# Four more attention units handled as one burst each, a new search of the order of work, and one store a half at the end of a Trainium2 attention and MoE kernel

## The chip, the cores and the metric

The kernel runs on one core of one Trainium2 chip. The metric is the device time of one execution in microseconds (us), as the median of several runs. The core has a matrix engine (TensorE, "PE" in the profile), a vector engine (DVE), a scalar engine (ACT), GpSimd (POOL) and a queue engine (SP), which here only issues DMAs. ACT also issues a few.

## The reference, cut to what matters

Random-feature attention over 8 batches of 8 heads with 576 tokens of 64 numbers and 128 features, and behind it a gated pair of projections:

```python
proj = np.einsum('bhsd,md->bhsm', x, omega)
h = proj - np.sum(x * x, axis=-1, keepdims=True) / 2.0
phi = np.exp(h - np.max(h, axis=-1, keepdims=True)) / np.sqrt(m)   # for q and for k
kv = np.einsum('bhsm,bhsd->bhmd', k_p, v)
z = np.sum(k_p, axis=2)
num = np.einsum('bhsm,bhmd->bhsd', q_p, kv)
den = np.einsum('bhsm,bhm->bhs', q_p, z)[..., None] + 1e-06
x = (num / den).transpose(0, 2, 1, 3).reshape(4608, 512)
out = ((x @ w_a) * (x @ w_b)) @ w_out        # w_a, w_b: 512 x 1536; w_out: 1536 x 512
```

## The kernel before, in words

**Two kinds of work on one matrix engine.** The attention is cut into 32 units, u = 4b + hp: batch b and pair of heads hp. So units 7 to 10 are (1,3), (2,0), (2,1) and (2,2). A unit projects k and q on the features (`four`, matmuls at L641 into `ppk` and `ppq`), forms kv (`kv_burst`, L918), and later the numerator (`num`, L990 for 512 tokens and L993 for the last 64). These matmuls use a part of the matrix engine's array at a time (the profile prints 64*64 or another shape behind the operation). The projections behind them ("MoE") run in 9 blocks of 512 tokens on the whole array (128*128): blocks 0 and 1 as plain matmuls (`moe_block`: L1327 for `pa` and `pb`, L1137 for the output `o`, 12 steps a block), blocks 2 to 8 by a scheme with sums of tiles and fewer products (`moe_block7`: the products at L1418 go into the banks `p0` and `p1` of PSUM, and DVE adds them at L1428). Each matmul is three: high and low halves of both operands, without low times low.

**The output of blocks 7 and 8** has the class `Out7`. Its products (L1206) collect in banks of their own, except for the product with key 1 (function `one`): this one goes into `p1`, DVE adds it to a sum in SBUF (`add`, L1216), and after that the next L1418 product may take `p1`. At the end of block 8 `store` writes four tiles `oc` of 128 x 512 numbers, the last one in two parts, as soon as each part has its last sum (L1213).

**What sets the order.** The program isn't in the order of its source. A planner (class `Graph`) collects all operations with their costs, and a list scheduler puts those of each engine in order by due times. Tables of numbers steer it: `PLACE` says at which MoE step a unit's matmuls stand, and `SHIFT` and `TILT` move single operations, by their number, in due time and in priority. `MERGED` lists units whose matmuls stand together: such a unit's burst takes the two banks that the next step's `pa` and `pb` will use (`pab`), holds its numerator of the unit ahead, kv and the projections, and goes to PE as one piece with MoE matmuls ahead and behind. A unit that isn't merged has several smaller pieces between MoE matmuls. In `JOIN` are units whose numerator is cut in two halves to share banks with kv. `LOWP` lists weight conversions of which one step is done by POOL. `XL` gives the steps from which the 64-token tails of all batches (block 8's x) may be loaded and split. `mm()` is the planner's price of a matmul.

**Stores.** A DMA is described by nested dimensions on both sides. The sums of the attention, `zx`, are stored 28 times to `zdr` as 8 rows of 32 numbers (L443, called from L893); each tile `oc` of the end in rows of 256 numbers.

Of the kernel before, what the change touches and what calls it, by code (L numbers as in the profile page):

```python
# [18 lines left out]
P = 128  # L19
B, H, S, D, M = 8, 8, 576, 64, 128  # L20
NHP = H // 2
NU = B * NHP
E, FF = H * D, 1536
# [3 lines left out]
HM = SM // 2  # L27
NFP = NF // 2
B1 = 2
TL = S - SM  # L30
# [6 lines left out]
EPS = 1e-6 * M  # L37
KS = NHP

CFG = dict(TWIN=(0, 1, 2, 3, 4, 6, 7), LOWP=(1, 6, 10, 12, 13, 16, 19, 20, 21, 22, 25, 33, 34), SQP=('natk_0_0', 'natk_0_1', 'natq_0_0', 'natq_0_1', 'natq_0_3'), BW=365.0, DLAT=(1500, 2600), QUEUE=8, XL=(0, 2), JOIN=(6, 7, 8, 9, 10), LOWD=430, SQB=1, GLUE=700, TURNS=99, EDF=("DVE", "ACT", "POOL"), ROUNDS=1, SQUEEZE=1, CAP=("DVE", "ACT", "POOL"), ZS=600, ZB=(1500, 3000, 5000), ZD=(1500, 3000, 4500), HQ=(2500, 4000, 5000), BACK2=(1500, 2500, 4000), TW=(), WAIT=0, RAW=2000, FAST=(0, 1, 2, 3), JOIN0=False, WARM=8, HROOM=["w0", "u1", "w1", "u2", "w2", "u3"], H=3, TURN=(7,), BACK=1500, AT=2, MERGED=(5, 12, 13, 14, 15, 16, 17, 18, 19, 20, 21, 22, 23, 24, 25, 26, 27, 28, 29, 30, 31), SQPE=4, MARGIN=1200, LOAD=2500, SUMS=1400, NATS=(2,), CONV=(22000, 2200))  # L40


PLACE = {4: 3, 5: 4, 6: 7, 7: 9, 8: 10, 9: 12, 10: 14, 11: 18, 12: 20, 13: 21, 14: 27, 15: 29, 16: 33, 17: 35, 18: 38, 19: 41, 20: 45, 21: 47, 22: 50, 23: 54,
         24: 58, 25: 59, 26: 62, 27: 66, 28: 67, 29: 70, 30: 74, 31: 77, 32: 78, 33: 83}


SHIFT = {49: -8000, 89: 1500, 99: -4000, 123: 500, 156: -4000, 179: -1000, 253: 9500, 459: -1000, 558: -2000, 629: 500, 633: -500, 646: -4000, 730: 8000, 749:
         8000, 989: 4500, 995: -8000, 1081: 4000, 1200: 8000, 1207: 4000, 1339: 4000, 1352: 5000, 1483: -8000, 1546: 8000, 1587: 3000, 1957: -8000, 2016:
         1500, 2248: -2000, 2395: -8000, 2854: 3500, 3508: -4000, 3860: -2000, 3940: 6000, 4192: 2000}
TILT = {15: 800, 19: -800, 21: 800, 30: 3000, 34: -800, 58: 3000, 75: -3000, 79: 800, 81: 800, 88: -3000, 105: 800, 109: -800, 115: -3000, 124: 3000, 135:  # L50
# [9 lines left out]


class Buf:
# [35 lines left out]
class Graph:  # L98
# [79 lines left out]
    def dues(self):  # L178
# [16 lines left out]
        for o in self.order:  # L195
            if "PE" in o.eng:
                idle += max(0, o.start - at - 5) * CFG["SQUEEZE"]
                at = o.end
# [11 lines left out]
        while heap:  # L210
            d, _, o = heapq.heappop(heap)
            e = next(iter(o.eng))
            cost = o.end - o.start if o.bytes else o.eng[e]
            if e in CFG["CAP"]:
                now = min(-d, ptr.get(e, inf))
# [12 lines left out]
    def plan(self):  # L228

        self.schedule()  # L230
        for _ in range(CFG["ROUNDS"]):
            self.dues()
            self.schedule()
        for o in self.ops:
            o.shift, o.tilt = SHIFT.get(o.n, 0), TILT.get(o.n, 0)
        self.schedule()
# [9 lines left out]
    def schedule(self):  # L246
# [12 lines left out]
        def entry(o, x, t):  # L259

            t = max(t, free[x] + 112 * (x == "DVE" and o.port == twice == 2))
            if x == "DVE" and o.port and port["POOL"][0] < t:
                t = max(t, port["POOL"][1] - 135)
            elif x == "POOL" and port["DVE"][0] <= t:
                t = max(t, port["DVE"][1] - 140)
            return t
# [20 lines left out]
        while len(done) < len(self.ops):  # L287
            best = None
            for e in engines:
                mine = None  # L290
                for o in ready[e]:
# [3 lines left out]
                    s = entry(o, e, max(o.need, at[0] + 92 * (e == "PE" and at[0] > 0)))  # L295
                    if o.bytes and len(landed) >= CFG["QUEUE"]:
                        s = max(s, landed[-CFG["QUEUE"]] + 100)
                    for x in o.eng:
# [3 lines left out]
                    else:  # L302


                        wait = CFG["WAIT"] if e == "DVE" and 0 <= o.prio < 4000 else 0
                        pr = o.shift + (o.prio if o.due is None or e not in CFG["EDF"] else o.due)
# [45 lines left out]

def mm(n, cols):

    return n * (118.1 if cols == 256 else max(112, 6.9 + 0.4375 * cols))


def mm4(n, cols):
# [24 lines left out]
def tile_attention_moe(ctx: ExitStack, tc: tile.TileContext, kqt, kqtt, kqn, kqnt, vx, omst, idn, wab, wout, out):  # L383
    nc = tc.nc
    SQPE = CFG["SQPE"]
# [10 lines left out]
    g = Graph()  # L396
# [45 lines left out]
    def dma(dst, src):  # L442
        return lambda e: nc.sync.dma_start(dst(), src())  # L443
# [63 lines left out]
    for kind, i, ws in units:  # L507
        n = place[kind, i, ws[0]]
# [26 lines left out]
        if kind == "o":  # L535
# [3 lines left out]
                 nbytes=P * 2 * E * 4)  # L539
# [570 lines left out]
    class Out:  # L1110
# [20 lines left out]
        def mm(self, t, ghl, wo, prio):  # L1131
            b, po, osb, n, h = self.b, self.po[t], self.osb[t // 2], self.n[t], t % 2
            self.n[t] += 1

            def go(e):
                for i, (gi, wi) in enumerate(((0, 0), (0, 1), (1, 0))):
                    nc.tensor.matmul(po.ap[:], ghl.ap[:, gi, t * P:(t + 1) * P], wo.ap[:, wi],  # L1137
                                     start=(n == 0 and i == 0), stop=(n == NF - 1 and i == 2))
            g.op({"PE": mm(3, E)}, go, r=[(ghl, None), (wo, None)], w=[(po, None)], alloc=[po] if n == 0 else [], prio=prio)
            if n < NF - 1:  # L1140
                return
            g.op({"ACT": act(E), "DVE": dve(E)}, copier(lambda: osb.ap[:, h], lambda: po.ap[:]), r=[(po, None)], w=[(osb, h)], alloc=[] if h else [osb], prio=-5)
            g.op({"SP": 330}, dma(lambda: out[b * S + t * P:b * S + (t + 1) * P, :], lambda: osb.ap[:, h]), r=[(osb, h)], prio=-5, nbytes=P * E * 4)
# [26 lines left out]
    class Out7:  # L1170
# [48 lines left out]
        def store(self, o, th, dh, part=None):  # L1219

            b, cols = self.b, slice(HM * dh, HM * dh + HM)
            if b < B:
                r0 = b * S + HM * th
                g.op({"SP": 330}, dma(lambda: out[r0:r0 + HM, cols].rearrange("(t p) c -> p t c", p=P), lambda: o.ap[:]), r=[(o, None)], prio=-5,
                     nbytes=P * E * 4)
                return
            rows = out.rearrange("(n s) c -> n s c", s=S)[4 * th:4 * th + 4, SM:S, cols].rearrange("(t j) r c -> j r t c", j=2)
            tt = slice(0, 2) if part is None else slice(part, part + 1)
            for j, (eng, queue) in enumerate((("SP", nc.sync), ("ACT", nc.scalar))):
                g.op({eng: 330}, lambda e, j=j, queue=queue: queue.dma_start(rows[j][:, tt], o.ap[TL * j:TL * j + TL, tt]),  # L1230
                     r=[(o, part)], prio=-5, nbytes=TL * E * (4 if part is None else 2))

        def items(self, i, C, ghl, Sg, wo, ot):

# [279 lines left out]
    def bursts(step, place, banks):  # L1514

        for u, at in PLACE.items():
            if at == step:
# [5 lines left out]
    for b in range(B + 1):  # L1523
        if b < B1:
            moe_block(b)
        else:
            if b == B:

                for hp in range(NHP):
# [3 lines left out]
                         prio=-20, nbytes=P * SM * 4, deps=[steps[NF * (B - 1) + CFG["XL"][0]]])  # L1533
# [88 lines left out]
```

## Time and profile before

| what | value |
|---|---|
| time, median of 3 runs | 1020.82 us (1020.35 to 1022.02) |
| profiled execution, its own time | 1018.96 us |
| its span | 1017.2 us |
| PE busy | 1006.6 us, 99% |
| DVE busy | 873.1 us, 86% |
| ACT, POOL busy | 574.6 us, 110.7 us |
| granted TensorE clock, mean | 0.999 |

The span is what the trace covers; the execution's time is 1.76 us longer, and the median of the runs 1.86 us longer than that execution. A row of the timeline gives start and length of an instruction or of several alike, and in brackets how long the engine had been idle before and what ended it.

### The profile page before, as it was taken

How to read it: one execution, taken by the hardware profiler on the slowest of the kernel's cores; microseconds unless marked ns; L12 is line 12 of the kernel's file. 1: busy time of each engine (PE TensorE's matmuls, PEld its weight loads, DVE VectorE, ACT ScalarE, POOL GpSimd, SP SyncE). 2: the span in 40 equal slices, each digit the busy share in tenths (PEclk: the TensorE clock that was granted, in tenths of full speed). 3: DMA queues.
4: the chain of work that ended last, by engine and by line, in shares of the span. 5: the costliest groups of instructions: out<-in, count | busy, mean ns of one | idle time of the engine just before them, and what ended most of it. 6: DMA issues, size and time to landing. Idle time of an engine off the chain costs nothing.

```text
span 1017.2 us, 27457 instructions
## 1 busy us (share of the span) xinstructions
PE 1006.6 (99%) x10538; PEld 890.0 (87%) x10538; DVE 873.1 (86%) x2162; ACT 574.6 (56%) x1584; POOL 110.7 (11%) x157
## 2 busy tenths in 40 slices
PE   9999999999999999999999999999999999999998
PEld 7777777777888999889988988988998999999997
DVE  7999999899997989877896889888887578999776
ACT  7998797667755647655663656575554024232221
POOL 0131212100111111110210111111110000000000
PEclk9999999999999999999999999999999999999999
DMA  9777887898999999999899889988887889999991
GB/s 356 289 268 256 284 258 223 302 337 306 307 332 383 308 311 303 330 321 312 269 317 357 285 288 328 335 286 294 279 300 256 295 290 347 315 354 337 374 328 44
DMA packets 123428, 306.76 MB, mean 302 GB/s; under 512 B 17952, under 2 KB 41248, under 8 KB 123296
## 3 DMA queue, kind: packets, MB, share of 16 engines
q1 hardware_dynamic: 122416, 304.34, 86.6%
q8 instruction: 83, 1.36, 0.6%
q10 hardware_dynamic: 880, 0.66, 0.2%
q14 instruction: 49, 0.40, 0.1%
HBM read 249.60 MB, written 55.34 MB: 300 GB/s over the span
## 4 chain that ended last, share of the span: by engine, by line
PE 92%; DVE 5%; DMA 1%; ACT 1%; issue 1%; SPq 0%; DVEq 0%; ACTq 0%
PE p L1418 39%; PE o L1137 23%; PE pb L1327 6%; PE pa L1327 6%; PE o_P L1206 5%; PE pkv L918 3%; PE ppk L641 3%; PE p L641 2%; PE p L990 2%; DMA X<-in_kqt_dram 1%; PE p L1206 1%; DVE sm L667 1%; PE ppq L641 1%; DVE raw L490 1%; PE pm L990 1%
## 5 line engine op out<-in xcount | busy, mean ns | idle before, releaser
L1428 DVE TENSOR_TENSOR c<-p,c 128x512 f32<-128x512 f32 (+1 forms) x336 | 208.0, 619 | 63.7 <-PE p L1418 60.7
L1137 PE MATMUL o<-wo,ghl 128*128 128x512 f32 x1008 | 255.9, 395 | 0.2 <-issue 0.2
L1137 PEld LDWEIGHTS o<-wo,ghl 128*128 128x128 f32 x1008 | 180.9, 188 | 38.5 <-issue 5.4
L1418 PE MATMUL p<-x,w 128*128 128x256 f32 x1008 | 136.2, 281 | 0.3 <-DVE c L1428 0.2
L1418 PEld LDWEIGHTS p<-x,w 128*128 128x128 f32 x1008 | 130.6, 189 | 6.6 <-DVE c L1428 0.9
L1418 PE MATMUL p<-Sa,t 128*128 128x256 f32 x1008 | 128.5, 276 | 0.0
L1418 PEld LDWEIGHTS p<-Sa,t 128*128 128x128 f32 x1008 | 121.0, 188 | 0.1
L432 ACT COPY c<-p 128x256 f32<-128x256 f32 x84 | 31.0, 369 | 115.1 <-PE p L1418 103.9
L948 ACT ACTIVATE hq<-hq,dn 128x128 f32<-128x128 f32 x224 | 69.7, 391 | 29.5 <-DVE dn L944 29.2
L865 POOL TENSOR_TENSOR z<-hk 128x256 f32<-128x256 f32 x28 | 25.2, 899 | 523.8 <-ACT hk L680 402.3
L1418 PE MATMUL p<-x,t 128*128 128x256 f32 x504 | 72.0, 278 | 0.8 <-DVE oc L1216 0.8
L938 DVE CUSTOM_DVE_ANT_0 zero<-hq,zb 128x128 bf16<-128x128 f32 x224 | 68.2, 304 | 4.1
L1418 PE MATMUL p<-Sb,bq 128*128 128x256 f32 x504 | 71.3, 277 | 0.0
L1418 PE MATMUL p<-Sb,t 128*128 128x256 f32 x504 | 71.0, 276 | 0.0
L680 ACT ACTIVATE hq<-hq,sm 128x128 f32<-128x128 f32 x196 | 64.7, 391 | 7.5 <-DVE sm L675 7.4
L1418 PEld LDWEIGHTS p<-x,t 128*128 128x128 f32 x504 | 64.8, 188 | 2.3 <-DVE oc L1216 1.0
L680 ACT ACTIVATE hk<-hk,sm 128x128 f32<-128x128 f32 x188 | 61.2, 391 | 8.2 <-DVE sm L675 8.1
L1418 PEld LDWEIGHTS p<-Sb,bq 128*128 128x128 f32 x504 | 63.9, 188 | 0.1
L1418 PEld LDWEIGHTS p<-Sb,t 128*128 128x128 f32 x504 | 63.6, 188 | 0.0
L432 ACT CAST ghl<-c 128x512 fp32r<-128x512 f32 (+1 forms) x60 | 32.8, 566 | 44.2 <-PE o L1137 25.8
L440 DVE TENSOR_TENSOR ghl<-c,ghl 128x512 fp32r<-128x512 f32 (+1 forms) x86 | 54.0, 641 | 4.2 <-ACT ghl L432 3.5
L1478 DVE TENSOR_TENSOR c<-c,c 128x512 f32<-128x512 f32 x82 | 55.5, 711 | 0.7
(245 smaller groups left out, 1898.4 us busy)
## 6 DMA issues: line engine op xcount, KB each, us to landing
t<-td SPq DMA_DIRECT2D x168, 512.0 KB
wo<-wod SPq DMA_DIRECT2D x96, 512.0 KB
bq<-bd SPq DMA_DIRECT2D x84, 256.0 KB
qdr<-qd SPq DMA_DIRECT2D x112, 144.0 KB
hq<-qdr SPq DMA_DIRECT2D x28, 576.0 KB
X<-in_kqt_dram SPq DMA_DIRECT2D x30, 512.0 KB
td<-ts SPq DMA_DIRECT2D x24, 512.0 KB
v<-in_vx_dram SPq DMA_DIRECT2D x28, 288.0 KB
```

The source lines that it names most:

```text
L432: nc.scalar.copy(o(), i())
L440: return lambda e: ENG[e].tensor_tensor(o(), i(), f(hi()), op=ALU.subtract)
L641: nc.tensor.matmul(flat4(pps[w])[half, c * M:c * M + M], x()[rows, c * P:c * P + P][:, half], om.ap[rows], start=True, stop=True)
L680: g.op({"ACT": 393 if b >= B1 or not own else 359}, lambda e, c=c, w=w, to=to, at=at: nc.scalar.activation(to.ap[:, at + c], src[w](c), AF ...
L938: g.op({"DVE": 302}, lambda e, c=c, qc=qc: nc.vector.tensor_tensor_reduce(out=junk.ap[:], in0=qc(), in1=zb.ap[:], scale=1.0, scalar=0.0, o ...
L948: g.op({"ACT": 392}, lambda e, c=c, src=src: nc.scalar.activation(hq.ap[:, c], src(), AF.Copy, scale=dn.ap[:, c:c + 1]), r=[sd, (dn, None) ...
L1137: nc.tensor.matmul(po.ap[:], ghl.ap[:, gi, t * P:(t + 1) * P], wo.ap[:, wi], start=(n == 0 and i == 0), stop=(n == NF - 1 and i == 2))
L1206: nc.tensor.matmul(pb.ap[:, t], A[0](ai)[:, t * P:(t + 1) * P], W[0](wi), start=begin and t == j == 0, stop=stop and t == 1 and j == 2)
L1327: nc.tensor.matmul(pb.ap[:], wt.ap[:, wi, c], xs[c].at(xi), start=(c == 0 and i == 0), stop=(c == NC4 - 1 and i == 2))
L1418: nc.tensor.matmul(pb.ap[:, half], wcol(wi, c), xc(xi, c), start=n == 0, stop=n == 5)
L1428: g.op({"DVE": dve(n)}, lambda e: nc.vector.tensor_tensor(c4.ap[:, o], pb.ap[:, half], y(), op=ALU.add), r=[*((pb, k) for k in range(half. ...
L1478: g.op({"DVE": dve(SM)}, lambda e, v=v, C=C: nc.vector.tensor_tensor(v(C[1]), v(C[1]), v(C[0]), op=ALU.mult), r=part, w=part[2:], prio=-10)
```

## The change

Units 7 to 10 are added to `MERGED`, and 7 to 10 leave `JOIN`. `LOWP` names 16 conversions in place of 13. The second number of `XL` is 1 in place of 2: block 8's x may be split one step earlier. `PLACE`, `SHIFT` and `TILT` have new numbers throughout, and the prices in `mm()` are a little lower. In `Out7.store` each part of the last tile goes out by one DMA of 128 rows (part 0 from SP, part 1 from ACT), where each part went out by two DMAs of 64 rows (one from SP, one from ACT). Lines behind 1232 have numbers higher by 6 in the changed kernel.

```diff
-CFG = dict(TWIN=(0, 1, 2, 3, 4, 6, 7), LOWP=(1, 6, 10, 12, 13, 16, 19, 20, 21, 22, 25, 33, 34), SQP=('natk_0_0', 'natk_0_1', 'natq_0_0', 'natq_0_1', 'natq_0_3'), BW=365.0, DLAT=(1500, 2600), QUEUE=8, XL=(0, 2), JOIN=(6, 7, 8, 9, 10), LOWD=430, SQB=1, GLUE=700, TURNS=99, EDF=("DVE", "ACT", "POOL"), ROUNDS=1, SQUEEZE=1, CAP=("DVE", "ACT", "POOL"), ZS=600, ZB=(1500, 3000, 5000), ZD=(1500, 3000, 4500), HQ=(2500, 4000, 5000), BACK2=(1500, 2500, 4000), TW=(), WAIT=0, RAW=2000, FAST=(0, 1, 2, 3), JOIN0=False, WARM=8, HROOM=["w0", "u1", "w1", "u2", "w2", "u3"], H=3, TURN=(7,), BACK=1500, AT=2, MERGED=(5, 12, 13, 14, 15, 16, 17, 18, 19, 20, 21, 22, 23, 24, 25, 26, 27, 28, 29, 30, 31), SQPE=4, MARGIN=1200, LOAD=2500, SUMS=1400, NATS=(2,), CONV=(22000, 2200))
+CFG = dict(TWIN=(0, 1, 2, 3, 4, 6, 7), LOWP=(0, 1, 4, 5, 6, 7, 10, 11, 12, 16, 20, 21, 25, 27, 33, 34), SQP=('natk_0_0', 'natk_0_1', 'natq_0_0', 'natq_0_1', 'natq_0_3'), BW=365.0, DLAT=(1500, 2600), QUEUE=8, XL=(0, 1), JOIN=(6,), LOWD=430, SQB=1, GLUE=700, TURNS=99, EDF=("DVE", "ACT", "POOL"), ROUNDS=1, SQUEEZE=1, CAP=("DVE", "ACT", "POOL"), ZS=600, ZB=(1500, 3000, 5000), ZD=(1500, 3000, 4500), HQ=(2500, 4000, 5000), BACK2=(1500, 2500, 4000), TW=(), WAIT=0, RAW=2000, FAST=(0, 1, 2, 3), JOIN0=False, WARM=8, HROOM=["w0", "u1", "w1", "u2", "w2", "u3"], H=3, TURN=(7,), BACK=1500, AT=2, MERGED=(5, 7, 8, 9, 10, 12, 13, 14, 15, 16, 17, 18, 19, 20, 21, 22, 23, 24, 25, 26, 27, 28, 29, 30, 31), SQPE=4, MARGIN=1200, LOAD=2500, SUMS=1400, NATS=(2,), CONV=(22000, 2200))
...
-PLACE = {4: 3, 5: 4, 6: 7, 7: 9, 8: 10, 9: 12, 10: 14, 11: 18, 12: 20, 13: 21, 14: 27, 15: 29, 16: 33, 17: 35, 18: 38, 19: 41, 20: 45, 21: 47, 22: 50, 23: 54,
...
+PLACE = {4: 3, 5: 4, 6: 7, 7: 8, 8: 10, 9: 11, 10: 15, 11: 16, 12: 20, 13: 21, 14: 27, 15: 31, 16: 33, 17: 35, 18: 39, 19: 41, 20: 46, 21: 47, 22: 52, 23: 54,
...
@@ -352,7 +352,7 @@
 
 def mm(n, cols):
 
-    return n * (118.1 if cols == 256 else max(112, 6.9 + 0.4375 * cols))
+    return n * (116.0 if cols == 256 else max(112, 6.9 + 0.4353 * cols))
 
 
 def mm4(n, cols):
@@ -1226,9 +1226,15 @@
                 return
             rows = out.rearrange("(n s) c -> n s c", s=S)[4 * th:4 * th + 4, SM:S, cols].rearrange("(t j) r c -> j r t c", j=2)
             tt = slice(0, 2) if part is None else slice(part, part + 1)
-            for j, (eng, queue) in enumerate((("SP", nc.sync), ("ACT", nc.scalar))):
+            queues = ("SP", nc.sync), ("ACT", nc.scalar)
+            if part is not None:
+                eng, queue = queues[part]
+                g.op({eng: 330}, lambda e: queue.dma_start(rows[:, :, tt], o.ap[:, tt]),
+                     r=[(o, part)], prio=-5, nbytes=P * HM * 4)
+                return
+            for j, (eng, queue) in enumerate(queues):
                 g.op({eng: 330}, lambda e, j=j, queue=queue: queue.dma_start(rows[j][:, tt], o.ap[TL * j:TL * j + TL, tt]),
-                     r=[(o, part)], prio=-5, nbytes=TL * E * (4 if part is None else 2))
+                     r=[(o, part)], prio=-5, nbytes=TL * E * 4)
 
         def items(self, i, C, ghl, Sg, wo, ot):
```

PE around unit 8, before: `o` and `pa0_10` are MoE matmuls of the whole array, the others (L990, L918, L641) the burst's.

```order
L1327 MATMUL pb0_9_2225<-x_0_1_637,wb9_2144 128x512 x3
L990 MATMUL pm_1_2_2241<-hq_1_2_1709,k2_1_2_1686 64x256 x2
...
L918 MATMUL pt_1_2_2242<-v_1_3_1957,htk2_2167 64x64
L1327 MATMUL pb0_9_2225<-x_0_2_768,wb9_2144 128x512 x3
...
L1137 MATMUL o0_2_1234<-wo7_1857,ghl0_7_2106 128x512 x3
L641 MATMUL ppk_2_00_2349<-om_75,X_2_0_1827 64x128
...
L641 MATMUL ppq_2_00_2350<-om_75,X_2_0_1827 64x128
L1137 MATMUL o0_3_1241<-wo7_1857,ghl0_7_2106 128x512 x3
...
L1327 MATMUL pa0_10_2386<-x_0_1_637,w10_2239 128x512 x3
L641 MATMUL ppk_2_04_2404<-om_75,X_2_0_1827 64x128
...
L641 MATMUL ppq_2_04_2405<-om_75,X_2_0_1827 64x128
L1327 MATMUL pa0_10_2386<-x_0_2_768,w10_2239 128x512 x3
```

The same place in the changed kernel, whose burst of unit 8 uses the banks `pab0` and `pab1` twice:

```order
L1137 MATMUL o0_2_1248<-wo8_1948,ghl0_8_2246 128x512 x3
L990 MATMUL pab0_0_10_2311<-hq_1_2_1734,k2_1_2_1719 64x512 x2
L993 MATMUL pab1_0_10_2312<-hq_1_2_1734,k2_1_2_1719 64x64 x2
L918 MATMUL pkv_2_00_2321<-v_1_3_2025,hk_2_0_2033 64x64
...
L918 MATMUL pkv_2_01_2322<-v_1_3_2025,htk2_2126 64x64
L641 MATMUL pab0_0_10_2371<-om_75,X_2_0_1851 64x128
...
L641 MATMUL ppk_2_04_2399<-om_75,X_2_0_1851 64x128
...
L641 MATMUL ppq_2_04_2400<-om_75,X_2_0_1851 64x128
L1333 MATMUL pa0_10_2425<-x_0_0_460,w10_2231 128x512 x3
```

Three visits of the unit's matmuls between MoE matmuls became one, and `pa0_10` follows directly on the burst.

PE in block 7 where the product with key 1 has a wait ahead of the next L1418 product, before: the L1206 rows into `p1` are that product, `o7_P2` another of the output.

```order
L1418 MATMUL p0_4299<-Sb_7_1_12097,t7_201_12327 128x256 x3
L1206 MATMUL o7_P2_12370<-wo7_3_12262,ghl7_3_12542 128x256 x6
L1206 MATMUL p1_4300<-wo7_2_12342,ghl7_2_12551 128x256 x6
L1418 MATMUL p1_4300<-x_7_2_11643,t7_201_12327 128x256 x3
L1418 MATMUL p1_4300<-x_7_3_12010,t7_201_12327 128x256 x3
```

And changed:

```order
L1424 MATMUL p0_4290<-Sb_7_1_12116,t7_201_12344 128x256 x3
L1206 MATMUL p1_4291<-wo7_2_12293,ghl7_2_12553 128x256 x6
L1206 MATMUL o7_P2_12368<-wo7_3_12146,ghl7_3_12550 128x256 x6
L1206 MATMUL o7_P4_12382<-ot7_11_12567,ghl7_3_12550 128x256 x6
L1424 MATMUL p1_4291<-x_7_2_11849,t7_201_12344 128x256 x3
L1424 MATMUL p1_4291<-x_7_3_12049,t7_201_12344 128x256 x3
```

Two products of six matmuls now stand between the key-1 product and the next one into `p1`, where there was none.

SP's last rows before (ACT has the same four stores): behind the names stands the shape of the store's destination, slowest dimension first; `x2` are the two parts.

```order
L443 DMA t_511_14222<-td_120 128x1024
L443 DMA bq_51_14244<-bd_132 128x512
L1230 DMA out_dram<-oc_0_13599 64x2x256
L1230 DMA out_dram<-oc_1_14444 64x2x256
L1230 DMA out_dram<-oc_2_14452 64x2x256
L1230 DMA out_dram<-oc_3_14467 64x256 x2
```

And changed (ACT again has the same four):

```order
L443 DMA t_511_14220<-td_120 128x1024
L443 DMA bq_51_14242<-bd_132 128x512
L1236 DMA out_dram<-oc_0_13598 64x2x256
L1236 DMA out_dram<-oc_1_14442 64x2x256
L1236 DMA out_dram<-oc_2_14450 64x2x256
L1232 DMA out_dram<-oc_3_14465 2x64x256
```

The last tile's store is one row on each queue, and its slowest dimension is 2, where it was 64.

## Rows read from the trace of the kernel before

**Rows 1.** The profile's page: busy time by engine, and shares of the last chain.

```profile
PE 1006.6 (99%) x10538; PEld 890.0 (87%) x10538; DVE 873.1 (86%) x2162; ACT 574.6 (56%) x1584; POOL 110.7 (11%) x157
PE 92%; DVE 5%; DMA 1%; ACT 1%; issue 1%; SPq 0%; DVEq 0%; ACTq 0%
```

**Rows 2.** Waits of PE, 10 rows in all: us in total, times, longest.

```profile
PE p L1418 <- DVE oc L1216: 0.8, 1, 0.8
```

**Rows 3.** Timeline of PE, two windows (the second begins at 142.9 us).

```profile
141.26 2.24 PE L1137 MATMUL o<-wo,ghl 128*128 128x512 f32 x9
...
142.65 0.86 PE L1137 MATMUL o<-wo,ghl 128*128 128x512 f32 x3
143.44 0.32 PE L641 MATMUL ppk<-om,X 64*64 64x128 f32 x1
...
144.14 0.27 PE L641 MATMUL ppk<-om,X 64*64 64x128 f32 x1
...
144.25 0.27 PE L641 MATMUL ppk<-om,X 64*64 64x128 f32 x1
...
144.47 0.96 PE L1137 MATMUL o<-wo,ghl 128*128 128x512 f32 x3
```

**Rows 4.** Timeline of PE, 863 to 868 us.

```profile
863.18 0.88 PE L1206 MATMUL p<-wo,ghl 128*128 128x256 f32 x6
864.84 0.96 PE L1418 MATMUL p<-x,t 128*128 128x256 f32 x6 [0.79 <-DVE oc L1216]
...
867.38 0.85 PE L1418 MATMUL p<-x,w 128*128 128x256 f32 x5 [0.19 <-DVE c L1428]
```

**Rows 5.** Timeline of DVE, 864 to 865 us.

```profile
864.10 0.69 DVE L1216 TENSOR_TENSOR oc<-p,oc 128x512 f32<-128x512 f32 x1
```

**Rows 6.** Timeline of PE around the merged burst of unit 5.

```profile
75.88 1.10 PE L641 MATMUL pab<-om,X 64*64 64x128 f32 x32
...
77.79 1.65 PE L1137 MATMUL o<-wo,ghl 128*128 128x512 f32 x6
79.28 2.03 PE L1327 MATMUL pa<-x,w 128*128 128x512 f32 x8
```

**Rows 7.** Timeline of ACT around the merged burst of unit 5.

```profile
77.66 0.56 ACT L432 COPY hk<-pab 128x512 f32<-128x512 f32 x1
...
78.92 0.57 ACT L432 COPY hq<-pab 128x512 f32<-128x512 f32 x1
```

**Rows 8.** Busy time by engine from 40 to 300 us, the sum of 13 stretches.

```profile
sum 260.00, PE 258.81 PEld 204.15 DVE 248.72 ACT 202.31 POOL 49.14; mean PE 19.91 PEld 15.70 DVE 19.13 ACT 15.56 POOL 3.78
```

**Rows 9.** Timeline of all engines from 1012.2 us (SPq and ACTq: issues of DMAs).

```profile
1012.26 0.76 DVE L1213 TENSOR_TENSOR oc<-p,oc 128x256 f32<-128x256 f32 x2
1012.96 1.21 SPq L1230 DMA_DIRECT2D out_dram<-oc  x2
1013.00 1.46 ACTq L1230 DMA_DIRECT2D out_dram<-oc  x2
```

**Rows 10.** Stretches: length, busy PE, PEld, DVE, ACT, POOL, clock, DMA share, GB/s.

```profile
850.00:855.00 5.00, 5.00 (x47) 5.00 (x46) 0.95 (x2) 0.76 (x2) 0.00 (x0) 1.00 1.03 387
...
1014.00:1015.00 1.00, 0.00 (x0) 0.00 (x0) 0.00 (x0) 0.00 (x0) 0.00 (x0) 1.00 0.98 292
1015.00:1016.00 1.00, 0.00 (x0) 0.00 (x0) 0.00 (x0) 0.00 (x0) 0.00 (x0) 0.51 0.46 140
```

**Rows 11.** DMA view: packets by size, and 4 of 38 rows of issues (866 issues).

```profile
DMA packets 123428, 306.76 MB, mean 302 GB/s; under 512 B 17952, under 2 KB 41248, under 8 KB 123296
...
t<-td SPq DMA_DIRECT2D x168, 512.0 KB
...
xtd<-xts SPq DMA_DIRECT2D x8, 128.0 KB
...
zdr<-zx SPq DMA_DIRECT2D x28, 1.0 KB
...
ident<-in_idn_dram ACTq DMA_DIRECT2D x1, 64.0 KB
```

More of the change, by code (lines that the diff above doesn't have):

```diff
@@ L43 @@
-PLACE = {4: 3, 5: 4, 6: 7, 7: 9, 8: 10, 9: 12, 10: 14, 11: 18, 12: 20, 13: 21, 14: 27, 15: 29, 16: 33, 17: 35, 18: 38, 19: 41, 20: 45, 21: 47, 22: 50, 23: 54,
[L44 to L49, printed above, removed]
@@ L50 @@
-TILT = {15: 800, 19: -800, 21: 800, 30: 3000, 34: -800, 58: 3000, 75: -3000, 79: 800, 81: 800, 88: -3000, 105: 800, 109: -800, 115: -3000, 124: 3000, 135:
[9 rows of a table removed]
+CFG = dict(TWIN=(0, 1, 2, 3, 4, 6, 7), LOWP=(0, 1, 4, 5, 6, 7, 10, 11, 12, 16, 20, 21, 25, 27, 33, 34), SQP=('natk_0_0', 'natk_0_1', 'natq_0_0', 'natq_0_1', 'natq_0_3'), BW=365.0, DLAT=(1500, 2600), QUEUE=8, XL=(0, 1), JOIN=(6,), LOWD=430, SQB=1, GLUE=700, TURNS=99, EDF=("DVE", "ACT", "POOL"), ROUNDS=1, SQUEEZE=1, CAP=("DVE", "ACT", "POOL"), ZS=600, ZB=(1500, 3000, 5000), ZD=(1500, 3000, 4500), HQ=(2500, 4000, 5000), BACK2=(1500, 2500, 4000), TW=(), WAIT=0, RAW=2000, FAST=(0, 1, 2, 3), JOIN0=False, WARM=8, HROOM=["w0", "u1", "w1", "u2", "w2", "u3"], H=3, TURN=(7,), BACK=1500, AT=2, MERGED=(5, 7, 8, 9, 10, 12, 13, 14, 15, 16, 17, 18, 19, 20, 21, 22, 23, 24, 25, 26, 27, 28, 29, 30, 31), SQPE=4, MARGIN=1200, LOAD=2500, SUMS=1400, NATS=(2,), CONV=(22000, 2200))
@@ new lines @@
+PLACE = {4: 3, 5: 4, 6: 7, 7: 8, 8: 10, 9: 11, 10: 15, 11: 16, 12: 20, 13: 21, 14: 27, 15: 31, 16: 33, 17: 35, 18: 39, 19: 41, 20: 46, 21: 47, 22: 52, 23: 54,
+         24: 57, 25: 59, 26: 62, 27: 64, 28: 67, 29: 70, 30: 74, 31: 79, 32: 81, 33: 83}
+SHIFT = {138: -9000, 822: 500, 965: 4000, 1013: -2000, 1084: 2000, 1120: -3000, 1227: 8000, 1250: 2000, 1320: -4000, 1451: -1000, 1566: 12000, 1590: -10500,
+         1757: -2000, 2546: -2000, 2581: 12000, 2583: 8000, 2993: -8000, 3326: 5000, 3455: -10000, 3553: 8000, 3675: 8000, 3778: -8500, 3780: -6500, 3809:
+         -4000, 3810: -3500, 3864: 500, 4710: -4000, 4807: 2000, 5014: 8000, 5040: -8000}
@@ L62 @@
+TILT = {19: -800, 21: -3000, 45: 3000, 49: 3000, 73: 3000, 75: 3000, 79: 3000, 94: -3000, 100: -3000, 115: -3000, 124: -800, 147: 3000, 160: 800, 173: 3000,
[9 rows of a table added]
 class Buf:
```

18 rows, old and new, of the table TILT are left out of this document.

## The prediction

> **What bounds the kernel now.** I read the page first. PE is busy for 1006.6 us of a span of 1017.2 us, and 92% of the chain that ended last is PE [rows 1]. So this kernel is made shorter only by fewer or cheaper matmuls, by taking away waits of PE, or by a shorter start and end. The list of PE's waits is short: ten rows, none over 1.0 us. One of them has a clear place in the order, the wait of an L1418 product for DVE's `oc` sum, 0.8 us [rows 2]. What a small change can take out of the middle is therefore some microseconds at most. I then looked at three places in the timeline: where PE goes from MoE matmuls to a unit's matmuls and back, the wait in block 7, and the end behind the last matmul.
>
> **The merged units.** The multiplications stay the same; a unit's matmuls only stand together. What changes is how often PE goes from whole-array matmuls to a unit's partial ones. Nine matmuls `o` begin at 141.26 us and the seventh of them at 142.65, so one takes 0.232 us. From there to the first `ppk` at 143.44 the last three take 0.79 us, 0.095 more than three times 0.232. On the way back a group of four projections takes 0.11 us (144.14 to 144.25), but from the last group to `o` 0.22 us pass: 0.11 more [rows 3]. So a visit costs about 0.2 us beside its work. Counted in the orders of PE's rows, units 7 to 10 make 13 visits before (4, 3, 3, 3) and 5 after (2, 1, 1, 1), and over the whole program the changes of array form are 167 before and 153 after, which is seven visits fewer. 7 x 0.2 = **-1.4 us**. It is between 0, if DVE sets the pace there (below), and -1.6 with all eight.
>
> **What merging adds.** A merged burst holds the two banks that the next `pa` and `pb` need, and these must first be copied out. Unit 5, merged already, shows how long: its last use of the banks begins at 75.88 us and lasts 1.10, other projections follow, and PE is back at MoE at 77.79 [rows 6]. ACT's copies out of the banks run from 77.66 to 78.22 and from 78.92 to 79.49 [rows 7]. Nothing waited, since six `o` stand between the burst and `pa` at 79.28 [rows 6]. In the changed order `pa` follows directly on the bursts of units 8 and 9. With ACT as late as for unit 5, `pa` would wait from 77.79 to 78.22, which is 0.43 us a burst; if the bank that it needs is the one copied second, 1.70 us (77.79 to 79.49). With an earlier copy it is nothing. `pb` comes 12 matmuls (2.8 us) later and is safe. The bounds are 0 and 2 x 1.70 = 3.4 us; I take half of the two short waits, **+0.4 us**, since ACT is not full and the planner knows the dependence.
>
> **The wait in block 7.** The key-1 product begins at 863.18 us, DVE adds it from 864.10 to 864.79 [rows 5], and the next product into `p1` begins only at 864.84, after 0.79 us of idle PE; a small wait of 0.19 us follows at 867.38, for DVE again [rows 4]. In the new order two products of six matmuls stand in between. The six matmuls from 863.18 need about 0.7 us, so twelve cover 1.4 us, where the sum needs 0.9 us from the product's end. I count the 0.79 and the 0.19 as gone: **-1.0 us**. DVE could still be behind: it is full from 860 us on, though between 850 and 855 it is busy for 0.95 us of 5 [rows 10], and the earlier split of block 8's x (`XL`) lets the scheduler put such work there. If it stays behind, the term is 0; an earlier key-1 product of the block has only one product behind it in place of two, which could give 0.25 back. The lower `mm()` prices, `SHIFT`, `TILT` and `LOWP` act only through the order. The remaining waits of PE may shift either way; I count them as nothing, within 2 us.
>
> **The last two stores.** The last sums end at 1013.02 us. Then SP issues two stores in 1.21 us and ACT two in 1.46 us, up to 1014.46 [rows 9]. In the change each issues one: SP's is done by about 1013.6 and ACT's by about 1013.75 (half of 1.46 behind 1013.02), which is 0.7 us earlier. If the data move at the same rate, the end is 0.7 us earlier as well. But the new store's destination begins with a dimension of 2, where all others of the end begin with 64. Does that alter how many DMA engines share it? The trace has one store with a small first dimension: `zdr`, 8 rows of 32 numbers, 28 times. The counts of the packets tell. There are 866 issues in the list, and 17952 packets under 512 B. Small data are `zdr`, 28 x 8 = 224 packets of 128 B, and `xtd`, 8 x 128 KB in pieces of 256 B (64 tokens of 4 B) = 4096. The rest is 13632, and 866 x 16 is 13856: short by 224 = 28 x 8 [rows 11]. This comes out to the packet if each DMA ends with one small packet on every engine that it uses, and all use 16 except the `zdr` stores, which use 8. So a first dimension of 8 means 8 engines, and by the same pattern one of 2 means two.
>
> [...]
>
> On two engines the price is this. Both stores hold 2 x 128 x 1024 B = 262 kB. An engine's rate is 292 / 16 / 0.98 = 18.6 GB/s in the stretch from 1014 us, and 387 / 16 / 1.03 = 23.5 GB/s from 850 us [rows 10]. If both stores use the same two engines, 262 kB take between 262 / 47.0 = 5.6 and 262 / 37.2 = 7.0 us; I take 6.3. Before, the last 262 kB were the 140 of 1015 to 1016 us and 122 of the 292 kB ahead [rows 10], so they began at about 1014.6 and ended at about 1015.6 (the engines are busy for 46% of that microsecond). With issues earlier by some 0.4 us at their start the new ones begin at about 1014.2 and end at 1020.5: **+4.9 us** (4.2 to 5.6). Nothing hides it, as no engine has work behind it. If the two queues take different pairs of engines, half the time is needed: 1014.2 + 3.15 = 1017.35, +1.8 us. [...]
>
> **The sum.** -1.4 + 0.4 - 1.0 + 4.9 = +2.9 us. Against the profiled execution's 1018.96 us that is 1021.9; the median of the runs lies 1.86 above that execution, and so the forecast for a median is 1020.82 + 2.9 = **1023.7 us**.
>
> **The rivals.**
> - *The stores spread over 16 engines after all* (the other side): the last term is -0.7 in place of +4.9, and the sum -2.7: 1018.1 us. For it: in the last stretch that is full of stores they move at 292 GB/s [rows 10]. Against it: the count of `zdr`. It decides from the point where the last two stores take less than about 2.5 us; then no slowdown is left.
> - *Two different pairs of engines*: -1.4 + 0.4 - 1.0 + 1.8 = -0.2: 1020.6 us.
> - *DVE takes the gain of the merged units.* From 40 to 300 us DVE is busy for 248.72 of 260 us [rows 8]. The changed order has 13 DVE instructions more; at 873.1 / 2162 = 0.40 us [rows 1] that is 5.2 us more work where only 11.3 are free. If PE has to wait for DVE anyway, the 1.4 us aren't gained: 1025.1, and with the block-7 wait kept too 1026.1. For it: hardly any slack. Against it: PE's waits there are short although DVE is that full.
> - *Other waits go as well.* The plan as a whole was drawn anew; if the rest of PE's short waits goes too, another 2 to 3 us: about 1021.2.
> - *The bursts wait for their banks*: +3.4 in place of +0.4, 1026.7. Against it: for unit 5 the first copy began ahead of PE's return [rows 6, 7].
>
> **Chances.** A change of 0.2% (2 us) is about what a measurement tells from none: faster is under 1018.8, slower over 1022.9. Same two engines with the sum as above: 0.42 (mostly slower, 0.04 same). The same with DVE or bank waits taking the gain: 0.22, slower. The same with other waits gone: 0.14, nearly all within 0.2%. Different pairs: 0.06, same. Sixteen engines: 0.16, of which 0.11 faster. Together: slower 0.60, same 0.27, faster 0.13. The range from 1018.5 to 1026.2 leaves out about 0.10 below and 0.06 above; with two engines given, it would be 1020.5 to 1026.2.
>
> **What would show it.** Behind the last matmul the DMA share falls to about 2/16 = 0.12 at some 40 GB/s for 5 to 6 us, and the time from the last sum to the span's end grows from 4.2 (1017.2 less 1013.02) to about 9 us. The time up to the last sum falls by about 2 us: bursts of units 7 to 10 in one piece with at most 0.4 us idle behind them, and no 0.79 us wait in block 7. The prediction is wrong if the DMA share stays near 1 to the end, if the matmuls end later than before, or if they end over 4 us earlier.

## The result, and the profile after

The changed kernel takes 1027.18 us (median of 6 runs, 1024.22 to 1029.42) against 1021.27 us before (6 runs in the same comparison). The ratio is 1.0056, with a 95% interval of 1.0035 to 1.0077: slower by 3.6 to 7.9 us. The forecast was slower, at 1023.7 us, and its range ended at 1026.2. The profiled execution of the changed kernel took 1029.34 us, near the top of that spread, which matters below.

The page of the changed kernel, busy time and last chain (these answer to [rows 1]):

```profile
PE 1007.1 (98%) x10522; PEld 891.8 (87%) x10522; DVE 881.2 (86%) x2175; ACT 563.7 (55%) x1565; POOL 112.1 (11%) x161
PE 82%; DVE 10%; DMA 2%; ACT 2%; issue 1%; SPq 1%; DVEq 0%; ACTq 0%
```

PE works as long as before, in a span of 1027.4 us in place of 1017.2. So nearly all of the 10.2 us are time in which PE waits or has nothing left to do. The tail comes first. The timeline of the changed kernel behind the last matmul, as in [rows 9]:

```profile
1017.01 0.76 DVE L1213 TENSOR_TENSOR oc<-p,oc 128x256 f32<-128x256 f32 x2
1017.71 0.58 SPq L1232 DMA_DIRECT2D out_dram<-oc  x1
1017.80 1.33 ACTq L1232 DMA_DIRECT2D out_dram<-oc  x1
```

And its stretches (length, busy time of PE, PEld, DVE, ACT and POOL, clock, DMA share, GB/s), as in [rows 10]:

```profile
1019.00:1020.00 1.00, 0.00 (x0) 0.00 (x0) 0.00 (x0) 0.00 (x0) 0.00 (x0) 1.00 0.46 135
1020.00:1021.00 1.00, 0.00 (x0) 0.00 (x0) 0.00 (x0) 0.00 (x0) 0.00 (x0) 1.00 0.12 34
...
1024.00:1025.00 1.00, 0.00 (x0) 0.00 (x0) 0.00 (x0) 0.00 (x0) 0.00 (x0) 0.50 0.14 48
1025.00:1026.00 1.00, 0.00 (x0) 0.00 (x0) 0.00 (x0) 0.00 (x0) 0.00 (x0) 0.50 0.11 40
```

From the last sum (1017.77) to the end of the span (1027.4) it is 9.6 us, and it was 4.2. For six microseconds the DMA share is 0.11 to 0.15, about 2/16. That is two DMA engines, and it explains 5.4 of the 10.2 us. The other 4.75 us were lost ahead of the last sum, which ends at 1017.77 in place of 1013.02. Not all of this lies between the kernels: the profiled execution of the kernel before was 2.3 us below the median of 1021.27, and this one is 2.2 us above its own. The list of PE's waits has:

```profile
PE pab L641 <- issue: 2.7, 1, 2.7
PE ps L656 <- ACT x L650: 1.7, 1, 1.7
PE ppk L641 <- ACT k L432: 1.2, 2, 0.7
...
PE p L1424 <- DVE c L1434: 0.4, 1, 0.4
```

The wait for the `oc` sum of [rows 2] is gone, as forecast. In its stead stands a wait of 2.7 us for "issue", which means that the profile shows nothing that PE waited for. Its place is the merged burst of unit 13 (3,1). PE's timeline there:

```profile
265.98 0.34 PE L641 MATMUL pab<-om,X 64*64 64x128 f32 x4 [2.71 <-issue]
267.26 4.55 PE L1137 MATMUL o<-wo,ghl 128*128 128x512 f32 x12
```

And the stretches around it:

```profile
262.00:264.00 2.00, 1.27 (x61) 1.03 (x53) 1.93 (x12) 1.28 (x6) 0.00 (x0) 1.00 1.07 312
264.00:266.00 2.00, 0.02 (x4) 0.02 (x4) 2.00 (x12) 0.00 (x0) 0.00 (x0) 1.00 0.76 239
266.00:268.00 2.00, 2.00 (x41) 1.70 (x42) 1.08 (x4) 0.00 (x0) 0.00 (x0) 0.79 0.18 56
268.00:270.00 2.00, 2.00 (x7) 1.52 (x6) 0.00 (x0) 0.00 (x0) 0.00 (x0) 0.50 0.72 209
270.00:272.00 2.00, 2.00 (x9) 1.64 (x8) 1.12 (x2) 1.77 (x5) 0.00 (x0) 0.86 0.63 109
```

PE stands still for the whole of 264 to 266 us, and then the granted clock is 0.50 from 268 to 270 us, the lower of the two values that this trace has (the other is 1.00): seven `o` matmuls follow one another every 0.43 us there, where 0.23 is usual. By the clocks 0.79, 0.50 and 0.86 of the three stretches, the lower level lasted some 3.4 us, in which eight matmuls begin that usually need 1.8. So this one wait costs 2.7 us and some 1.6 us more behind it, 4.3 in all. The six executions of this kernel lie between 1024 and 1029 us; whether this wait is in each of them, and how long, the single trace can't say. Their mean granted clocks suggest that the stretch at 0.50 isn't in each: three have 0.995, like this one, one has 0.996, and two have 0.997 (1024.22 and 1026.03 us), as much as the profiled execution of e2 below, whose clock falls only behind the last matmul. What this wait is and what it costs became the question of the experiments, beside the end.

### The profile page after: what moved, and what is told of

It is laid out like the page before. It is cut to its first block, busy times and chain, and to the rows that moved or that the text cites. A ratio compares the mean times of both kernels' runs of the same rounds, so it can differ in the third digit from the quotient of the medians.

```text
span 1027.4 us, 27390 instructions
## 1 busy us (share of the span) xinstructions
PE 1007.1 (98%) x10522; PEld 891.8 (87%) x10522; DVE 881.2 (86%) x2175; ACT 563.7 (55%) x1565; POOL 112.1 (11%) x161
## 2 busy tenths in 40 slices
DMA packets 123366, 306.73 MB, mean 299 GB/s; under 512 B 17892, under 2 KB 41188, under 8 KB 123236
## 4 chain that ended last, share of the span: by engine, by line
PE 82%; DVE 10%; DMA 2%; ACT 2%; issue 1%; SPq 1%; DVEq 0%; ACTq 0%
PE p L1424 39%; PE o L1137 20%; PE o_P L1206 5%; PE pb L1333 4%; PE pa L1333 4%; PE pkv L918 3%; PE p L641 2%; PE ppk L641 2%; PE p L990 2%; DVE raw L490 2%; DVE sm L667 1%; DVE zero L938 1%; DMA X<-in_kqt_dram 1%; PE p L1206 1%; DVE sq L621 1%
## 5 line engine op out<-in xcount | busy, mean ns | idle before, releaser
L948 ACT ACTIVATE hq<-hq,dn 128x128 f32<-128x128 f32 x224 | 71.8, 394 | 40.7 <-DVE dn L944 40.6
L680 ACT ACTIVATE hq<-hq,sm 128x128 f32<-128x128 f32 x200 | 66.8, 392 | 5.8 <-DVE sm L675 5.7
L865 POOL TENSOR_TENSOR z<-z,hk 128x256 f32<-128x256 f32 x56 | 45.5, 812 | 48.0 <-ACT hk L680 45.2
```

The lines of the kernel that those rows point to most:

```text
L680: g.op({"ACT": 393 if b >= B1 or not own else 359}, lambda e, c=c, w=w, to=to, at=at: nc.scalar.activation(to.ap[:, at + c], src[w](c), AF ...
L865: g.op({"POOL": pool2(n)}, lambda e: nc.gpsimd.tensor_tensor(o(), a(), c(), op=ALU.add), r=r, w=w, alloc=list(al), prio=pri, deps=zload[-1 ...
L948: g.op({"ACT": 392}, lambda e, c=c, src=src: nc.scalar.activation(hq.ap[:, c], src(), AF.Copy, scale=dn.ap[:, c:c + 1]), r=[sd, (dn, None) ...
```

## The experiments

Each run below is compared with runs of the kernel before on the same chip, in five rounds. In the first texts the burst at 261 us is called unit 12's; it is unit 13's, and what is called unit 11's near 249 us is unit 12's.

| run | plan | last stores | median us | before us | ratio (95%) |
|---|---|---|---|---|---|
| e1_old_stores | changed | old | 1021.60 | 1020.75 | 1.0007 (0.9993 to 1.0020) |
| e2_before_new_stores | before | new | 1026.16 | 1020.75 | 1.0050 (1.0035 to 1.0066) |
| e3_two_dmas_one_queue | changed | 64 rows each, one queue a half | 1021.66 | 1020.75 | 1.0006 (0.9993 to 1.0019) |
| e4_pad64_rows | changed, PE's stream moved by 64 | old | 1024.62 | 1021.16 | 1.0037 (1.0021 to 1.0052) |
| e5_pad128_rows | changed, moved by 128 | old | 1026.10 | 1021.16 | 1.0047 (1.0027 to 1.0066) |
| e6_xl_back | changed, XL (0, 2) | old | 1023.22 | 1021.16 | 1.0019 (1.0008 to 1.0030) |
| e7_hold_loads | changed, four loads later | old | 1019.27 | 1021.47 | 0.9982 (0.9970 to 0.9993) |
| e8_hold_both | changed, six loads later | old | 1023.67 | 1021.47 | 1.0022 (1.0012 to 1.0033) |

**The two halves of the change apart (e1, e2).** e1 is the changed kernel with the stores of before:

```diff
-            queues = ("SP", nc.sync), ("ACT", nc.scalar)
-            if part is not None:
-                eng, queue = queues[part]
-                g.op({eng: 330}, lambda e: queue.dma_start(rows[:, :, tt], o.ap[:, tt]),
...
+            for j, (eng, queue) in enumerate((("SP", nc.sync), ("ACT", nc.scalar))):
```

> The changed kernel with the old last stores: each half again as two DMAs of 64 rows, one from each queue; all the rest of the order as changed. Theory (the end: two half stores on two DMA engines cost some 5.3 us, of 9.6 less 4.2 us from the last sum to the end of the span; the rest of the plan is worth little): the time falls by 5.0 to 5.6 us against the changed kernel, to a median of about 1021.8, within 1.5 us of the kernel before, and the stretch from the last sum to the end is 4.2 us again. Rival (the plan's own waits of PE are the loss, above all the wait of 2.7 us in unit 12's burst with the half clock behind it): it stays over 1024, since only an end hidden behind late work was changed.

e2 is the kernel before with that edit the other way round.

> The kernel before with the new last stores alone. Theory of the end: +5.0 to +5.6 us, a median of 1026.2 to 1026.9, and DMA share 0.12 with 35 to 48 GB/s for some 6 us at the end. Rival (the plan is the loss): within 2 us of the kernel before.

The stores alone cost 5.1 us (3.6 to 6.7, the ratio times 1020.75), which is nearly the whole difference, and the plan without them is worth 0.7 us, slower (-0.7 to 2.0), not told from nothing. From the last sum to the end it is 9.6 us in e2's trace and 4.3 in e1's. Where the last sum ends is less telling: e2 has the plan of before, and its last sum ends at 1016.03 us, 3.0 us behind that of the trace of before. By so much two executions of one plan differ. The end of e2:

```profile
1019.00:1020.00 1.00, 0.00 (x0) 0.00 (x0) 0.00 (x0) 0.00 (x0) 0.00 (x0) 0.80 0.12 44
...
1023.00:1024.00 1.00, 0.00 (x0) 0.00 (x0) 0.00 (x0) 0.00 (x0) 0.00 (x0) 0.50 0.14 48
```

**One queue or two engines (e3).** Each half still goes out from its one queue, but as two DMAs whose slowest dimension is 64:

```diff
-                g.op({eng: 330}, lambda e: queue.dma_start(rows[:, :, tt], o.ap[:, tt]),
+                g.op({eng: 660}, lambda e: [queue.dma_start(rows[j][:, tt], o.ap[TL * j:TL * j + TL, tt]) for j in range(2)],
```

> The changed kernel; each half still goes out from one queue (part 0 SP, part 1 ACT), but as two DMAs of 64 rows, whose slowest dimension is 64. If the first dimension of 2 is what makes the stores slow: as fast as with the old stores within 0.7 us (the second issue of a queue comes some 0.6 us later), about 5 us below the changed kernel. If it is that each half has one queue only: no gain, within 1 us of the changed kernel.

1.0006: as fast as with the old stores, and 4.3 us from the last sum to the end. So the queue a half is innocent, and the first dimension of 2 is what costs. The packets say the same. In the traces of e2 and of the changed kernel both queues' counts fall by 30 against before (the two data queues, packets and MB of the changed kernel; before they had 122416 and 880):

```profile
q1 hardware_dynamic: 122386, 304.34, 86.1%
q10 hardware_dynamic: 850, 0.66, 0.2%
```

On each queue two DMAs of 64 rows, 2 x (64 + 16) = 160 packets, became one of 128 rows, and 128 + 2 = 130 is 30 fewer. With 16 engines it would be 144. In e3's trace the 30 are back on both:

```profile
q1 hardware_dynamic: 122416, 304.34, 86.2%
q10 hardware_dynamic: 880, 0.66, 0.2%
```

Of the packets under 512 B there are 17892 in e2 and in the changed kernel and 17952 before, so all 60 of both queues are small ones. A slowest dimension of 2 went with two engines here, as the 8 of `zdr` goes with eight by the count of [rows 11]. From 1022 to 1025 us of the changed kernel packets of both queues are under way and the share is 0.12 to 0.14, so both used the same two.

**What PE waits for (e4, e5).** In the traces of before, e1, e2, e3 and the changed kernel every longer wait for "issue" of PE was laid beside two things. First, a queue that the profile calls "instruction" (q8): it brings packets of 16 KB, and each of these waits ends 1.2 to 1.6 us behind the end of one. In the changed kernel the packet begins at 263.55 us, after PE has stopped, and takes 1.09 us; PE goes on at 265.98. Second, the place of the waiting matmul in PE's stream, counted over weight loads, matmuls and semaphore instructions: 5568 and 9152 in the kernel before, 5825 and 13505 in the changed plan. All these are 192 or 193 above a multiple of 256. The instruction queue brought 82 packets in the changed kernel, for 21157 instructions of PE: one for every 258. So PE's instructions seem to come in blocks of 256, and the wait is for the next block. To test it, one-column matmuls on zeros were put behind the warm-up, 32 in e4 and 64 in e5; all engines keep their order:

```diff
         for _ in range(CFG["WARM"]):
             nc.tensor.matmul(none.ap[:], zero.ap[:], zero.ap[:, 0:1].to_broadcast([P, SM]), start=True, stop=True)
+        for _ in range(32):
+            nc.tensor.matmul(none.ap[:, 0:1], zero.ap[:], zero.ap[:, 0:1], start=True, stop=True)
```

> The changed plan with the old last stores, and 32 more one-column matmuls on zeros at the start, which move everything behind them by 64 instructions in PE's stream; the order is the same on all engines. Theory (PE's instructions come in blocks of 256, and each wait that the profile puts down to issue stands at instruction 192 or 193 of 256, 1.2 to 1.6 us behind the end of a 16 KB packet of the instruction queue; a wait comes where 256 instructions run in few us while the data DMAs are full): the wait in unit 12's burst leaves its place (the 26th pab projection); the block ends now at 4.0 us apart just ahead, in unit 11's matmuls near 249 us, with a wait of 1 to 3 us there, and the wait near 610 us gets shorter or goes. Rival (the wait belongs to these instructions, by a bank or data not shown): it stays at the 26th projection with 1 to 3 us. Time within 2 us of the run with the old stores, beside up to 2 us for the added matmuls.

> The same with 64 one-column matmuls, 128 instructions. Theory of the instruction blocks: no wait of over 0.5 us at the 26th pab projection of unit 12's burst nor near 610 us, since the block ends fall elsewhere; but many bursts now run a whole block in 2.6 to 3.5 us (near 316, 369, 389, 540, 560, 637 us), and there waits of issue of up to 1 us come; the time is 1 to 6 us above the run with the old stores, beside up to 4 us for the added matmuls. Rival (bank or data): the waits stay at their places.

In both, the waits in unit 13's burst and near 610 us are gone, and others stand elsewhere. (The one near 610 us says little: it is 1.6 us long in the traces of e1 and e3, but the traces of the changed kernel and of e6 don't have it either.) PE's timeline of e4, the three rows with such a wait:

```profile
485.59 0.32 PE L643 MATMUL ppq<-om,X 64*64 64x128 f32 x1 [0.48 <-issue]
...
544.42 0.74 PE L1420 MATMUL p<-Sa,t 128*128 128x256 f32 x4 [0.57 <-issue]
...
658.56 0.45 PE L643 MATMUL p<-om,Xe 64*64 64x128 f32 x7 [1.43 <-issue]
```

And of e5, the three longest:

```profile
350.49 0.44 PE L643 MATMUL p<-om,Xe 64*64 64x128 f32 x6 [0.40 <-issue]
...
392.00 0.85 PE L1139 MATMUL o<-wo,ghl 128*128 128x512 f32 x3 [1.49 <-issue]
...
715.82 0.27 PE L643 MATMUL ppk<-om,X 64*64 64x128 f32 x1 [1.27 <-issue]
```

Counted in the same way, these stand at 10689, 11969 and 14785 in e4 and at 7616, 8640 and 16064 in e5: again 192 or 193 above a multiple of 256, with 64 and 128 more instructions ahead of them. The rival, a wait that belongs to the matmuls of that burst, has fallen. The wait of 1 to 3 us that was expected in e4 near 249 us did not come, and of the places named for e5 only some had one: the blocks' ends say where a wait can be, not that it is there. By the ratios both are slower than e1, e4 by 3.0 and e5 by 4.1 us, of which the added matmuls take 0.8 and 1.6 (the first projections begin at 5.33 and 6.10 us, in e1 at 4.52). Their runs spread from 1021 to 1030 and to 1032 us, and the profiled executions (1021.02 and 1023.67 us) lie low in it, so where the rest is lost was not seen. In part it may be the clock: the runs of 1028 us and more have a mean granted clock of 0.996 or 0.997, the two profiled ones 1.000.

**The other part of the plan that could be undone alone (e6).**

```diff
-XL=(0, 1)
+XL=(0, 2)
```

> The changed plan with the old last stores and XL set back to (0, 2): block 8's x is split a step later again. If the earlier split is what frees DVE for the key-1 sum in block 7: a wait of PE for DVE of 0.7 us or more comes back between 840 and 880 us, and the time is 0.5 to 1.5 us above the run with the old stores. If the new tables alone do it: no such wait, and the time within 0.5 us.

The waits are back in PE's list of e6:

```profile
PE p L1418 <- ACT oc L432: 0.7, 1, 0.7
...
PE p L1418 <- DVE oc L1216: 0.4, 1, 0.4
```

They stand at 855 and 870 us, in block 7, and the kernel is 1.2 us slower than e1 by the ratios, whose intervals overlap. The reading that the earlier split helps there is supported, not settled by the times.

**Why the block comes late (e7, e8).** A packet of the next block begins, in most places, over 100 instructions ahead of the block's end, and never over 295. At the end of the block in unit 13's burst it began some 115, 0 and 0 instructions ahead in e1, e3 and the changed kernel, 7 to 9 us after PE had passed the end of the block ahead. In that time the data queue filled the DMA engines. The DMA view of the changed kernel from 254.9 us (where PE passed that end) to 263.5 us, share of 16 engines:

```profile
q1 hardware_dynamic: 1301, 3.36, 102.7%
```

In e7 four loads that aren't needed there were moved on SP, behind the `zdr` store at 262 us; no other engine's order changes:

```diff
-    order = g.plan()
+    order = list(g.plan())
+    late = [o for o in order if o.n in (1850, 1872, 1899, 2073)]
+    order = [o for o in order if o not in late]
+    at = order.index(g.ops[1499]) + 1
+    order[at:at] = late
```

> The changed plan with the old last stores, and four loads that SP issues between 247 and 258 us (t, X, natq, t; 1.83 MB, not needed before 282 us) put behind the zdr store at 262 us; the order of all other engines is the same. (In earlier texts the burst at 261 us is called unit 12's; it is unit 13's.) Theory (the 16 KB packet with PE's next instructions starts late because the data DMAs ahead of it fill all engines at 400 GB/s until 262 us): the packet starts some 4 us earlier, the wait of issue of 1.1 to 2.5 us at the 26th pab projection goes or falls under 0.5 us, no matmuls at half clock follow, and the time falls by 1 to 3 us against the run with the old stores (median 1019 to 1020.5). Rival (the packet comes late whatever the data DMAs do): the wait stays over 1 us and the time is the same.

PE's timeline in e7's burst, and below it the stretch 260 to 262 us:

```profile
262.26 1.24 PE L641 MATMUL pab<-om,X 64*64 64x128 f32 x29
263.32 0.28 PE L641 MATMUL pab<-om,X 64*64 64x128 f32 x3
264.40 1.89 PE L1137 MATMUL o<-wo,ghl 128*128 128x512 f32 x7
```

```profile
260.00:262.00 2.00, 2.00 (x65) 1.33 (x68) 1.86 (x9) 1.26 (x4) 0.55 (x1) 1.00 0.04 8
```

For comparison, the wait of the same projection in the lists of e1 and of e3:

```profile
PE pab L641 <- issue: 1.1, 1, 1.1
```

```profile
PE pab L641 <- issue: 2.5, 1, 2.5
```

The 26th projection, which waited 1.1 to 2.7 us in e1, e3, e6 and the changed kernel, now follows its forerunner without a pause, and no matmul runs at half clock. It waits in none of the two traces with the four loads held back (e7, e8), and in all four of this plan and this count of instructions without that. The data queue is empty at 260 us (DMA share 0.04), and at 260.67 the block's packet begins, some 200 instructions ahead. The time is 0.9982 of the kernel before (0.9970 to 0.9993), 1.8 us faster, and 2.5 us below e1 by the two ratios (0.7 to 4.4 by their intervals). This is faster than both kernels of the change. In the size the expectation held; in the mechanism one number did not: the packet was to start some 4 us earlier, and did start 0.9 to 2.9 us earlier on the clock. In e7 it starts about half a microsecond behind the last data; in the other traces it starts while the DMA share is still between 0.8 and 1.0. So fewer data ahead bring the packet earlier, but what exactly it waits for is not shown.

The traces also tell where the time goes. PE does the same matmuls in the same order in e7, e1, e3 and the changed kernel, and up to block 7 in e6, so their starts can be laid side by side. From 262 to 270 us of e7 the changed kernel falls 4.3 us behind it, e3 4.1 and e6 3.8, each 1.6 us more than its wait of 2.7, 2.5 and 2.2, and each with a stretch at half clock; e1, which has none, falls behind by 1.1, which is its wait. From 270 to 600 us the first three keep that distance within 0.1 us, and e1 loses 1.1 more. So one trace doesn't give the time of a kernel: e1's, with the short wait, ended 2.1 us behind e3's, with the long one. Nor is the half clock in most runs. 3.4 us at 0.50 lower a run's mean granted clock by 0.0017, so a run at 0.999 or 1.000 can't have had it. Such are 6 of 12 runs of e1, 7 of e3 and 8 of e6, and all 12 of e7.

e8 holds back two more loads, X and natq, near 600 us, for the wait of 1.64 us near 610 us:

> The same, and two loads issued at 592 and 602 us (X and natq, 0.79 MB) put behind the zb loads at 610 us. Theory: the wait of issue near 610 us (1.64 us in two traces) falls below 1 us as well, and the time is 0 to 1.6 us below the run before this one. Rival: the wait at 610 us stays at 1.6 us, or the late X delays the projections near 616 us.

No wait for issue stands near 610 us there (one of 0.6 us does in e7), but it was absent from two traces without this edit as well, so its absence shows nothing. The kernel is slower, 1.0022. e8's timeline of ACT and of PE shows why:

```profile
613.95 0.63 ACT L615 ACTIVATE natq<-natq 128x512 f32<-128x512 f32 x1 [3.27 <-DMA natq<-in_kqn_dram]
614.49 0.35 ACT L432 COPY c<-p 128x256 f32<-128x256 f32 x1
```

```profile
614.89 1.65 PE L1418 MATMUL p<-Sa,t 128*128 128x256 f32 x6 [2.92 <-ACT c L432]
```

ACT stood for 3.27 us on the `natq` that was held back, and behind it in ACT's order stood a copy out of `p`, for which PE then waited 2.92 us. Behind this wait the granted clock was 0.50 as well, from 616 to 618 us (six L1418 products begin at 616.35 us and take 1.48 us, six from 619.24 take 0.84), and e8 is 3.8 us later against e7 at 615 us than at 606. The load had more time by its own consumer's due time than by what is queued behind that consumer.

## Why the prediction was right and wrong, point by point

**The last stores: right, and the cause as well.** +4.9 us was forecast, on two engines, from the count of the `zdr` packets in [rows 11]. Measured were 5.1 us by e2's ratio and 5.4 by the traces' ends. Rate and length were near (34 to 49 GB/s for about 6 us); the data only began later, some 2 us behind the last sum and not 1.2. ACT's single issue took 1.33 us, where half of 1.46 was counted. No row of before shows which engines the two queues take: that they take the same two was the author's estimate, and the share of 0.12 to 0.14 with both queues at work bears it out. The rivals of 16 engines and of different pairs are out.

**The merged units: the price of a visit was right.** Counted in PE's rows behind 62 us, the visits fall from 50 to 41, nine where seven were counted from the order. The median excess on the way in is 0.09 us and on the way out 0.09 (0.199 less 0.11), in both traces. So 9 x 0.18 = 1.6 us are saved by this count, for the 1.4 forecast; no run undid the merging alone, so the saving itself isn't measured.

**The bank waits behind bursts of units 8 and 9:** +0.4 was forecast; no wait of a `pa` or `pb` stands in the lists of the changed kernel, e1, e3, e6 or e7. The term is 0. A wait for a bank came at another place, `ppk` behind ACT's copy of `k` near 104 us, 0.7 to 1.1 us at the longest in each of these traces.

**Block 7: about right.** The 0.79 and 0.19 us of [rows 4] are gone; a wait for DVE of 0.4 to 0.6 us near 846 us is there in two traces of the plan and absent in two (e3, e7). The term is between -1.0 and -0.4.

**The step that failed** is this sentence: "The remaining waits of PE may shift either way; I count them as nothing, within 2 us." The plan as a whole was forecast at -2.0 us and measured at +0.7 (-0.7 to 2.0). What was put at nothing is the wait for instructions in unit 13's burst, in some executions with the half clock behind it: 1.1 us in e1's trace, 3.8 to 4.3 in three others. With that one wait taken away (e7), the plan is at -1.8 us (-3.1 to -0.7), about what was forecast for it. That the whole of the missing 2.7 us is this wait isn't shown, as its size changes from run to run. Of the prediction's own signs, those of the end came true, and that of the matmuls did not: the last sum ends at 1017.77 us and not some 2 us ahead of 1013.02. A sign of the wait stood in the list of before, in the burst at 249.7 us, and it was passed over as too small:

```profile
PE ppq L641 <- issue: 0.5, 1, 0.5
```

The rival that came nearest in size, DVE taking the gain (+1.4 to +2.4), named the wrong engine: DVE's 13 instructions more are there (881.2 us busy in place of 873.1), and PE's waits for DVE grew from 1.5 to 2.3 us in the lists, beside the 1.0 us at the start. But 1.8 us of such waits stand in e7 too, which has the forecast gain.

The forecast of 1023.7 us was low by 3.5, and the range's end at 1026.2 by 1.0. Of the 3.5 us, 2.7 belong to this step and 0.2 to the stores; 0.45 are the median of before, which was 1020.82 us when the forecast was made and 1021.27 in the comparison.

## What to carry to other kernels

Before merging two stores into one, look at the slowest dimension of the destination: stores that start with a 2 used two engines here and cost 5.1 us at the end of the kernel, where nothing hid that. When matmuls are packed more closely, ask what feeds the engine besides data: a wait for "issue" in the list, however small, can mark a place where the instructions themselves come late, as the one of 0.5 us did in the list of before, and here it was longest, 2.7 us, where many short instructions ran while the data queue stood at 102.7% of the engines' time. Holding back four loads there gave 2.5 us, where the new order alone gave none that can be told; whether it would help the kernel before was not run. But a load's slack is that of everything queued behind its consumer, as e8 shows.

## What the runs showed of the hardware that was not expected

PE's waits for "issue" that were counted, ten in all, stand at 192 or 193 above a multiple of 256 in its stream, and end 1.2 to 1.6 us behind a 16 KB packet of the instruction queue. In the changed kernel that queue brought one such packet for every 258 of PE's instructions. In unit 13's burst the packet began 8.6 us behind the end of the block ahead, with the data queue at 102.7% of the engines' time, and with 1.83 MB of loads held back (e7) 5.8 us behind it. And after PE had stood for 2.7 us, the granted clock was 0.50 for some 3.4 us, though PE had resumed with full work. The same was seen behind waits of 2.2 us (e6), 2.5 us (e3) and 2.9 us (e8, where PE had waited for ACT and not for instructions); behind waits of 1.1 us (e1), 1.4 us (e4), 1.5 us (e5) and 1.6 us (e1 and e3, near 610 us) no such stretch was seen.
